# Block 0's rows turned by VectorE, two indirect writes in unit 20, earlier table steps, and the last x's transposes between up products

## The chip, the cores and the metric

The kernel runs on one core of one Trainium2 chip. The metric is the device time of one execution in microseconds (us), from the runs' own clock; a profile of one more execution gives the trace. A core has TensorE (matrix products and transposes, results in PSUM), VectorE and ScalarE (which read and write SBUF and PSUM), GpSimd (SBUF only; it also issues the indirect DMAs) and SyncE, whose queue issues all the direct DMAs. In the rows they are PE, DVE, ACT, POOL and SP.

## What is computed

Two steps follow each other. The first is a linear attention with a decaying state (B=4, H=8, S=768, D=48), computed in the kernel chunk by chunk:

```
for t in range(S):
    cur = einsum('bhd,bhe->bhde', u[None] * kt, vt)
    y[:, :, t] = einsum('bhd,bhde->bhe', rt, state + cur)
    state = wt[:, :, :, None] * state + einsum('bhd,bhe->bhde', kt, vt)
x = y.transpose(0, 2, 1, 3).reshape(3072, 384)
```

The second is a mixture of experts over the 3072 rows of x (8 experts, 384 to 1024 to 384), each row going to one expert:

```
logits = x @ w_gate + modality_bias[modality_id]
e_idx = argmax(logits, axis=1);  gate_w = softmax(logits)[e_idx]
for e in range(E):
    h = maximum(x[mask] @ w1[e], 0.0)
    out[mask] = gate_w[mask, None] * (h @ w2[e])
```

## The kernel before

**Attention.** The 3072 rows are 24 units of 128. A loop `for i in range(-2, NU)` (NU = 24) is a hand-made pipeline: iteration i prepares unit i+2 (decay products B and E, then K and G), makes the scores of unit i+1 (`pS`, masked into `A`) and the result of unit i (`pY`, in the last iteration `pU`). `x_rows(n)` adds `dV` and writes unit n's rows into `xp`; `x_cols(n)` transposes them on TensorE into `pT` or `pK`, from where ScalarE copies them to `xT`; `logits(n)` multiplies by w_gate into the PSUM tile `T["R"]` (`pR_x` in the rows). The program is written out by hand: each engine works through its instructions in the order in which the code issues them, and waits by semaphores.

**Routing.** The rows are routed in two parts, units 0 to 9 (while attention still runs) and 10 to 23. Once the places of the first part are known, `hook_b(0)` puts ten scatters into `pend`, and `drain(1)` issues one indirect write of 128 rows into the DRAM buffer `xs` at the end of each iteration on GpSimd's queue. `table(0)` is a generator whose steps, small operations on VectorE within `pR_x`, find out which expert the blocks 0 and 1 belong to; `hooks` call its steps (`tb`) at the end of the last two iterations.

**Blocks.** The experts' work runs over blocks of 512 rows. `rows_load(q)` loads a block's rows from `xs` into `xl`; for block 0 this is one DMA with 128 rows on the partitions, and its wait is for the last scatter of the first part. In the last iteration `blk_t(0)` turns block 0 by twelve transposes of TensorE into `pX`, `pK` and `pY`, ScalarE casts each third to `xh` and VectorE makes the remainder `xo = x - xh`, since each fp32 product is made of three fp32r products (`xh·wh`, `xo·wh`, `xh·wl`). Blocks from 1 on come by four DMAs of 32 partitions and are turned by VectorE (`rows_turn`, a 32x32 stream transpose) into `xt` in SBUF. The weights of the first expert are split the same way: `w_split_half` casts an eighth's half on ScalarE to `wh` and makes `wl` on GpSimd, sixteen pieces of 128x192 in all. `blk_up(q, f)` is one of eight up products, nine matmuls into a PSUM bank, followed by relu on ScalarE (`h`) and its remainder on VectorE; block 0 uses the two banks `pS0` and `pS1` in turn, later blocks three (`pS0`, `pS1`, `pT`). `blk_down` follows with 72 matmuls. Work of the second routing part stands between the products of block 0, `logits(NU - 1)` after the third (`s == 2`).

Of the kernel before, what the change touches and what calls it, by code (L numbers as in the profile page):

```python
# [18 lines left out]
P = 128  # L19
# [41 lines left out]
def kernel(ctx: ExitStack, tc: tile.TileContext, rkw, vt, wf, cst, mid, wg, bias, w1, w2, out):  # L61
# [223 lines left out]
    SPLITS = {NU - 2: 4, NU - 1: 8}  # L285
    BY_TWO = (1, 2, 7, 8, 9, 10, 11)

    def att_iter(i):
# [21 lines left out]
        if ok(z - 1):  # L310
            x_rows(z - 1, i in BY_TWO)
        last = first(m + 1)
# [78 lines left out]
        if i == NU - 1:  # L391
            x_rows(z)
            blk_t(0)
            x_cols(z, pt(("x", 1), "pT"))
            logits(z - 1)
        if i >= NU - 2:
            hooks.pop(0)()
# [260 lines left out]
    def rows_load(q, at, nj):  # L658
# [4 lines left out]
        if q == 0:  # L663
            nc.sync.dma_start(out=xl.rearrange("p a c -> p (a c)").rearrange("p (j c) -> p j c", j=JT),
                              in_=src[:, 0:DM].rearrange("(j p) c -> p j c", p=P))
        for i in range(4 if q else 0):
            nc.sync.dma_start(out=xl[32 * i:32 * i + 32, 0:4 * nj], in_=src[:, XC * i:XC * i + XC].rearrange("(b t) c -> t b c", t=32))
# [8 lines left out]

    def blk_t(q):
        w = width(q)
        X["x", q] = [bp["m"].tile([P, KC, BT], dt, tag=nm, name=f"{nm}{q}", bufs=1) for nm, dt in (("xh", F32R), ("xo", F32R), ("xt", F32))]
        if q == 0:  # L680
            bp["m"].tile([P, 56], F32, name="pad1")
        xg = X["xg", q]
        xh, xo, xt = ([t[:, m, 0:w] for m in range(KC)] for t in X["x", q])
        if q == 0:
            xl = X["xl", q].rearrange("p a c -> p (a c)").rearrange("p (j k m) -> p j m k", j=JT, m=KC)
            xt = [pt(f"x0_{m}", t) for m, t in enumerate(("pX", "pK", "pY"))]
            for m in range(KC):
                for j in range(JT):
                    nc.tensor.transpose(out=xt[m][:, j * P:(j + 1) * P], in_=xl[:, j, m], identity=ident)

        def rest(m):
            nc.vector.tensor_tensor(out=xo[m], in0=xt[m], in1=xh[m].bitcast(F32), op=ALU.subtract)

        for m in range(KC):
            if q:
                rows_turn(q, m, w // 32, xt[m])
            nc.scalar.copy(out=xh[m], in_=xt[m])
            if m:
                rest(m - 1)
        rest(KC - 1)  # L700
        nc.vector.reciprocal(out=xg[:, :, 0:1], in_=xg[:, :, 0:1])
# [480 lines left out]
```

## Time and profile before

| | |
|---|---|
| timed runs | median 333.74 us, 333.08 to 336.19 (3 runs) |
| the profiled execution | 332.86 us, of which the span (first to last instruction) 331.1 us |
| TensorE busy | 319.8 us, 97% of the span |
| VectorE, ScalarE, GpSimd busy | 222.0, 204.0 and 195.0 us: 67, 62 and 59% |
| granted TensorE clock | 0.999 of full speed |
| DMA | 66.22 MB, mean 200 GB/s |

Attention takes the first 120 us of the span, then come the blocks. Times in the rows are us from the span's start; a matmul row's duration contains the pipeline, so the work of one is read from the distance to the next row's start. Short transfers of 512 B and less make up 27569 of 48321 DMA packets.

### The profile page before, as it was taken

The page shows a single profiled execution, that of the slowest core. Times are in us where ns is not written, and L with a number is a line of the kernel's source. Part 1 is how long each engine was busy: PE and PEld are TensorE (multiplying, and loading weights), DVE is VectorE, ACT ScalarE, POOL GpSimd, SP SyncE. Part 2 cuts the span into 40 slices and gives each one's busy share as a digit, 9 for nine tenths or more (in the row PEclk, how much of TensorE's full clock was granted, in tenths as well). Part 3 has the DMA queues.
Part 4 walks back from the last instruction along what each step waited for, and adds up shares of the span by engine and source line. Part 5 has one row for each costly group of instructions (what it writes and reads, how often), then busy time and mean ns, then how long its engine had stood idle before and what let it go on. Part 6 is the DMA issues. An engine that isn't in the chain of part 4 may idle for free. (4 is left out here: it accounts for less than half of the span.)

```text
span 331.1 us, 9946 instructions
## 1 busy us (share of the span) xinstructions
PE 319.8 (97%) x3831; PEld 279.6 (84%) x3831; DVE 222.0 (67%) x382; ACT 204.0 (62%) x466; POOL 195.0 (59%) x226
## 2 busy tenths in 40 slices
PE   8899999999899999999999999999999999999993
PEld 3688999889799897888888888888888999889993
DVE  6999999899999746777514995874472465353220
ACT  3898799677588875642314748637775786524240
POOL 7998889879999975575435550652056233604041
PEclk9999999999999999999999999999999999999999
DMA  7998889967998532514778128945996594332011
GB/s 267 414 332 263 272 295 258 302 229 246 303 287 277 183 97 89 104 72 173 238 236 213 51 69 201 375 144 131 325 259 262 146 342 157 78 104 78 0 70 56
DMA packets 48321, 66.22 MB, mean 200 GB/s; under 512 B 27569, under 2 KB 34825, under 8 KB 48264
## 3 DMA queue, kind: packets, MB, share of 16 engines
q1 hardware_dynamic: 45160, 56.02, 55.0%
q0 software_dynamic: 3104, 9.47, 7.4%
q8 instruction: 32, 0.52, 0.6%
q14 instruction: 25, 0.20, 0.2%
HBM read 61.65 MB, written 16.46 MB: 236 GB/s over the span
## 5 line engine op out<-in xcount | busy, mean ns | idle before, releaser
L760 POOL DMA_INDIRECT out<-ot,xg x24 | 25.3, 1054 | 72.2 <-ACT ot L772 67.7
L228 ACT CAST wh<-raw 128x768 fp32r<-128x768 f32 x48 | 39.0, 830 | 32.3 <-PE pK_d L730 16.3
L229 POOL TENSOR_TENSOR wl<-raw,wh 128x768 fp32r<-128x768 f32 x20 | 38.8, 1953 | 28.5 <-ACT wh L228 28.4
L717 DVE SCALAR_TENSOR_TENSOR h<-pS_u,h 128x512 fp32r<-128x512 f32 (+1 forms) x34 | 22.9, 674 | 36.1 <-ACT h L716 30.9
L229 DVE TENSOR_TENSOR wl<-raw,wh 128x768 fp32r<-128x768 f32 x28 | 31.0, 1113 | 15.2 <-ACT wh L228 14.5
L711 PE MATMUL pS_u<-xh,wh 128*128 128x512 f32 (+1 forms) x102 | 39.7, 390 | 0.2 <-DVE h L717 0.2
L711 PE MATMUL pS_u<-xo,wh 128*128 128x512 f32 (+1 forms) x102 | 39.2, 384 | 0.0
L711 PE MATMUL pS_u<-xh,wl 128*128 128x512 f32 (+1 forms) x102 | 39.1, 384 | 0.0
L716 ACT ACTIVATE h<-pS_u 128x512 fp32r<-128x512 f32 (+1 forms) x34 | 19.8, 582 | 26.6 <-PE pS_u L711 22.5
L641 POOL DMA_INDIRECT xs<-xp,posT x24 | 24.5, 1022 | 11.2 <-issue 8.2
L246 POOL TENSOR_TENSOR K<-in,B 128x512 f32<-128x512 f32 x24 | 28.4, 1185 | 4.2 <-PE pK L321 2.3
L307 POOL TENSOR_TENSOR G<-in 128x512 f32<-128x512 f32 x24 | 30.6, 1274 | 0.0
L730 PE MATMUL pY_d<-h,wh 128*128 128x512 f32 (+1 forms) x80 | 30.5, 381 | 0.0
L730 PE MATMUL pX_d<-h,wh 128*128 128x512 f32 (+1 forms) x80 | 30.5, 381 | 0.0
L730 PE MATMUL pK_d<-h,wh 128*128 128x512 f32 (+1 forms) x80 | 30.5, 381 | 0.0
L296 DVE TENSOR_TENSOR_SCAN B<-in,pX_d 128x516 f32<-128x516 f32 x24 | 29.3, 1220 | 1.8 <-DMA in<-rkw 1.8
L299 DVE TENSOR_TENSOR_SCAN E<-in,pX_d 128x516 f32<-128x516 f32 x24 | 29.5, 1229 | 0.8
L386 PE MATMUL pY<-v,A 128*64 128x48 f32 x368 | 25.1, 222 | 0.0
L348 DVE TENSOR_TENSOR A<-pS,m 128x768 f32<-128x768 f32 x24 | 22.8, 948 | 2.9 <-PE pS L346 2.7
L252 ACT ACTIVATE pU_st<-pU_st,B 128x48 f32<-128x48 f32 x80 | 22.0, 275 | 3.0 <-PE pU_st L358 0.5
L386 PEld LDWEIGHTS pY<-v,A 128*64 128x64 f32 x368 | 23.7, 138 | 0.0
L346 PEld LDWEIGHTS pS<-R,K 64*64 64x64 f32 x768 | 18.6, 133 | 5.1 <-issue 4.2
(248 smaller groups left out, 829.6 us busy)
## 6 DMA issues: line engine op xcount, KB each, us to landing
raw<-w SPq DMA_DIRECT2D x24, 768.0 KB
in<-rkw SPq DMA_DIRECT2D x23, 512.0 KB
v<-vt SPq DMA_DIRECT2D x24, 288.0 KB
in<-rkw SPq DMA_DIRECT2D x23, 258.5 KB
wg<-wf SPq DMA_DIRECT2D x8, 576.0 KB
xl<-xs SPq DMA_DIRECT2D x20, 192.0 KB
raw<-w SPq DMA_DIRECT2D x16, 192.0 KB
yd<-yt SPq DMA_DIRECT2D x16, 192.0 KB
```

The source lines that it names most:

```text
L228: nc.scalar.copy(out=wh[k][:, sl], in_=raw[k][:, sl])
L229: (eng or (nc.vector, nc.gpsimd)[k]).tensor_tensor(out=wl[k][:, sl], in0=raw[k][:, sl], in1=wh[k][:, sl].bitcast(F32), op=ALU.subtract)
L246: nc.gpsimd.tensor_tensor(out=wt(a, "K", [P, 4, P]), in0=quarters(k), in1=quarters(T["B", a][:, 1:517])[:, :, 1:129], op=ALU.mult)
L296: nc.vector.tensor_tensor_scan(out=Bt[:, 516:0:-1], data0=w[:, 516:0:-1], data1=d1[:, 516:0:-1], initial=0.0, op0=ALU.mult, op1=ALU.max)
L299: nc.vector.tensor_tensor_scan(out=Et, data0=w[:, 0:516], data1=d1[:, 1:2].to_broadcast([P, 516]), initial=1.0, op0=ALU.mult, op1=ALU.max)
L307: nc.gpsimd.tensor_tensor(out=wt(a, "G", [P, 512]), in0=r, in1=k, op=ALU.mult)
L386: nc.tensor.matmul(out=yh[64:P, g, sw, hh], lhsT=A[:, hh, g, 1 + sw], rhs=vs[:, g, hh] if sw else v[:, h * D:(h + 1) * D], start=new and n ...
L641: rows_apart("xs", nc.gpsimd.indirect_dma_start(out=xs[:, :], out_offset=bass.IndirectOffsetOnAxis(ap=posT[:, n:n + 1], axis=0), in_=T["xp ...
L711: nc.tensor.matmul(out=pp, lhsT=wsrc[0][:, f, c * P:(c + 1) * P], rhs=xsrc[:, c], start=(n == 0), stop=(n == 3 * KC - 1))
L717: nc.vector.scalar_tensor_tensor(out=hl, in0=pp, scalar=0.0, in1=hh.bitcast(F32), op0=ALU.max, op1=ALU.subtract)
L730: nc.tensor.matmul(out=X["y", q][c][:, 0:width(q)], lhsT=wsrc[1][:, f, c * P:(c + 1) * P], rhs=hsrc, start=(first and n == 0), stop=(last ...
L760: ins = nc.gpsimd.indirect_dma_start(out=out[:, :], out_offset=bass.IndirectOffsetOnAxis(ap=xg[0:n, j, 1:2].bitcast(I32), axis=0), in_=ot[ ...
```

## The change

Five edits. (1) `rows_load(0)` uses the four DMAs of the other blocks, and block 0 is turned by VectorE in the last iteration, with the casts, three of the weight pieces and the remainders in a new order (`blk_x` takes `blk_t`'s parts apart). (2) Iteration 20 (`NU - 4`) issues two scatters, iteration 21 none. (3) The table's step 1 is called at the end of iteration 21, step 2 in iteration 22 ahead of the mask, the rest at the end of iteration 23. (4) The x columns and logits of unit 23, and the logits of unit 22, stand between the up products of block 0; up products of block 0 use three banks. (5) In the last iteration three weight pieces instead of eight stand ahead of the rest, and the splits for block 1's first weights are made after the up products 2, 3, 5 and 7 instead of 1, 3, 5 and 7.

```diff
-    SPLITS = {NU - 2: 4, NU - 1: 8}
+    SPLITS = {NU - 2: 4}
...
-        if ok(z - 1):
+        if i == NU - 1:
+            b0 = blk_x(0)
+            for c in range(KC):
+                if c == KC - 1:
+                    x_rows(z - 1)
+                rows_turn(0, c, NXB, b0.xt[c])
+                if c == KC - 1:
+                    for _ in range(3):
+                        w_split_half(next(done))
+                b0.cast(c)
+            for c in range(KC):
+                b0.rest(c)
+        elif ok(z - 1):
             x_rows(z - 1, i in BY_TWO)
+            if i == NU - 2:
+                next(tb)
...
             x_cols(z - 1, pt(("x", 0), "pT"))
-        if i == NU - 1:
             x_rows(z)
-            blk_t(0)
-            x_cols(z, pt(("x", 1), "pT"))
-            logits(z - 1)
-        if i >= NU - 2:
+            b0.gate()
             hooks.pop(0)()
...
-        if q == 0:
-            nc.sync.dma_start(out=xl.rearrange("p a c -> p (a c)").rearrange("p (j c) -> p j c", j=JT),
-                              in_=src[:, 0:DM].rearrange("(j p) c -> p j c", p=P))
-        for i in range(4 if q else 0):
+        for i in range(4):
             nc.sync.dma_start(out=xl[32 * i:32 * i + 32, 0:4 * nj], in_=src[:, XC * i:XC * i + XC].rearrange("(b t) c -> t b c", t=32))
...
+    class blk_x:
...
+        def cast(self, m):
+            nc.scalar.copy(out=self.xh[m], in_=self.xt[m])
+        def rest(self, m):
+            nc.vector.tensor_tensor(out=self.xo[m], in0=self.xt[m], in1=self.xh[m].bitcast(F32), op=ALU.subtract)
+        def gate(self):
+            nc.vector.reciprocal(out=self.xg[:, :, 0:1], in_=self.xg[:, :, 0:1])
...
-        pp = pt(f"u{q}_{f}", UPB[(ORDER.index(q) * FC + f) % 3] if isinstance(q, int) and q else f"pS{f % 2}", (P, BT))[:, 0:width(q)]
+        pp = pt(f"u{q}_{f}", UPB[(ORDER.index(q) * FC + f) % 3] if isinstance(q, int) else f"pS{f % 2}", (P, BT))[:, 0:width(q)]
...
-        if i >= NU - 2:
-            hooks.append(lambda n=1 + 2 * (i == NU - 1): [next(tb, None) for _ in range(n)])
+        if i in (NU - 3, NU - 1):
+            hooks.append((lambda: next(tb)) if i < NU - 1 else lambda: list(tb))
...
-        drain(1)
+        drain(2 if i == NU - 4 else 1)
...
-            if s == 2:
-                logits(NU - 1)
+            if s == 0:
+                x_cols(NU - 1, pt(("x", 1), "pT"))
+            if s in (1, 2):
+                logits(NU - 3 + s)
...
-            if q != 1 and f % 2 and nxt < HO:
+            if q > 1 and f % 2 and nxt < HO:
                 w_split(0, f // 2)
+            if q == 0 and f in (2, 3, 5, 7):
+                w_split(0, f // 2 - (f == 2))
```

How the instructions stand now, at three places. VectorE before, from the mask of unit 23 to the first step-2 operation (xp is x_rows, the five operations on pR_x and hd are the table's step 1, xo are the remainders of block 0 read from PSUM):

```order
L348 TENSOR_TENSOR A_2626<-pS_2627,m_111 128x768
L522 TENSOR_SCALAR pR_x<-pR_x 128x8
...
L526 SCALAR_TENSOR_TENSOR pR_x<-one_153,pR_x 128x8
L423 TENSOR_TENSOR xp_1426<-pY_2657,dV_2609 128x384
L423 TENSOR_TENSOR xp_1426<-pU_2718,dV_2699 128x384
L692 TENSOR_TENSOR xo_2753<-pX_x_0_2756,xh_2752 128x512
L692 TENSOR_TENSOR xo_2753<-pK_x_1_2757,xh_2752 128x512
L692 TENSOR_TENSOR xo_2753<-pY_x_2_2758,xh_2752 128x512
L701 RECIPROCAL xg_2597<-xg_2597 128x4
L578 TENSOR_SCALAR fs_2690<-pR_x 128x9
```

VectorE now, from the x rows of unit 21 on (fs to t2 is step 2, xt is block 0 turned in SBUF):

```order
L433 TENSOR_TENSOR xp_1426<-pY_2580,dV_2497 128x384
L588 TENSOR_SCALAR fs_2572<-pR_x 128x9
...
L561 TENSOR_TENSOR t2(0, 1)_2633<-pR_x,t2(0, 1)_2633 128x1
L362 TENSOR_TENSOR A_2650<-pS_2651,m_111 128x768
L679 STREAM_TRANSPOSE xt_2719<-xl_2604 128x512 x2
L433 TENSOR_TENSOR xp_1426<-pY_2681,dV_2620 128x384
L679 STREAM_TRANSPOSE xt_2719<-xl_2604 128x512
L697 TENSOR_TENSOR xo_2718<-xt_2719,xh_2717 128x512 x3
L433 TENSOR_TENSOR xp_1426<-pU_2737,dV_2715 128x384
L700 RECIPROCAL xg_2605<-xg_2605 128x4
L564 SCALAR_TENSOR_TENSOR pR_x<-pR_x,t2(0, 1)_2633 128x1
```

Step 2 moved ahead of the mask A, and the turning ahead of the x rows of units 22 and 23. TensorE before, from the logits of unit 21 to the first up product:

```order
L439 MATMUL pR_x<-cs,xT_2673 64x8 x6
L433 MATMUL pT_('x', 0)_2745<-cs,xp_1426 128x128 x3
L689 MATMUL pX_x_0_2756<-cs,xl_2596 128x128 x4
L689 MATMUL pK_x_1_2757<-cs,xl_2596 128x128 x4
L689 MATMUL pY_x_2_2758<-cs,xl_2596 128x128 x4
L433 MATMUL pT_('x', 1)_2778<-cs,xp_1426 128x128 x3
L439 MATMUL pR_x<-cs,xT_2746 64x8 x6
L711 MATMUL pS_u_0_2872<-xh_2752,wh_74 128x512
L711 MATMUL pS_u_0_2872<-xo_2753,wh_74 128x512
```

TensorE now, the same place up to the third up product:

```order
L449 MATMUL pR_x<-cs,xT_2697 64x8 x6
L443 MATMUL pT_('x', 0)_2764<-cs,xp_1426 128x128 x3
L720 MATMUL pS_u_0_2851<-xh_2717,wh_74 128x512
...
L720 MATMUL pS_u_0_2851<-xh_2717,wl_75 128x512
L443 MATMUL pT_('x', 1)_2864<-cs,xp_1426 128x128 x3
L720 MATMUL pS_u_1_2872<-xh_2717,wh_74 128x512
...
L720 MATMUL pS_u_1_2872<-xh_2717,wl_75 128x512
L449 MATMUL pR_x<-cs,xT_2765 64x8 x6
L720 MATMUL pT_u_2_2891<-xh_2717,wh_74 128x512
```

The twelve transposes are gone, the last x's transposes stand behind the first up product, and the logits of unit 22 behind the second. ScalarE before, from the copy of unit 21's x on (xh are the casts of block 0, wh the weight pieces, h the first relu):

```order
L434 COPY xT_2673<-pK_2672 128x384
L234 CAST wh_74<-raw_72 128x192 x8
L434 COPY xT_2746<-pT_('x', 0)_2745 128x384
L697 CAST xh_2752<-pX_x_0_2756 128x512
L697 CAST xh_2752<-pK_x_1_2757 128x512
L697 CAST xh_2752<-pY_x_2_2758 128x512
L434 COPY xT_2779<-pT_('x', 1)_2778 128x384
L234 CAST wh_74<-raw_72 128x192 x4
```

ScalarE now:

```order
L444 COPY xT_2697<-pK_2696 128x384
L694 CAST xh_2717<-xt_2719 128x512 x2
L234 CAST wh_74<-raw_72 128x192 x3
L694 CAST xh_2717<-xt_2719 128x512
L444 COPY xT_2765<-pT_('x', 0)_2764 128x384
L234 CAST wh_74<-raw_72 128x192 x9
```

Three weight casts stand between the second and the third cast of block 0, nine behind, and the first relu follows those nine.

## Rows read from the trace of the kernel before

**Rows 1.** Windows, one stretch: its length, then busy us of each engine

```profile
131.00:326.00 195.00, 195.00 (x951) 169.68 (x949) 105.95 (x200) 102.66 (x165) 80.63 (x79) 1.00 0.55 167
```

**Rows 2.** Timeline of TensorE, 116 to 131: start, us, engine, line, operation, idle before

```profile
116.79 0.50 PE L439 MATMUL pR_x<-cs,xT 128*64 128x8 f32 x12
...
119.16 0.25 PE L383 MATMUL pU<-vz,A 128*64 128x96 f32 x1
...
120.68 0.55 PE L433 MATMUL pT_('x', 0)_2745<-cs,xp 128*128 128x128 f32 x3
121.06 0.62 PE L689 MATMUL pX_x<-cs,xl 128*128 128x128 f32 x4
...
122.43 0.49 PE L433 MATMUL pT_('x', 1)_2778<-cs,xp 128*128 128x128 f32 x3
...
123.30 0.50 PE L711 MATMUL pS_u<-xh,wh 128*128 128x512 f32 x1
123.64 0.40 PE L711 MATMUL pS_u<-xo,wh 128*128 128x512 f32 x1
...
127.93 0.50 PE L711 MATMUL pS_u<-xh,wh 128*128 128x512 f32 x1 [0.21 <-DVE h L717]
...
129.87 0.39 PE L711 MATMUL pS_u<-xh,wl 128*128 128x512 f32 x1
...
130.64 0.50 PE L711 MATMUL pS_u<-xh,wh 128*128 128x512 f32 x1
```

**Rows 3.** Timeline of VectorE, 113 to 127

```profile
113.94 0.56 DVE L423 TENSOR_TENSOR xp<-pY,dV 128x384 f32<-128x384 f32 x1 [1.13 <-PE pY L386]
115.22 0.96 DVE L348 TENSOR_TENSOR A<-pS,m 128x768 f32<-128x768 f32 x1 [0.72 <-PE pS L346]
...
124.22 0.14 DVE L578 TENSOR_SCALAR fs<-pR_x 128x9 f32<-128x9 f32 x1
...
126.45 0.16 DVE L551 TENSOR_TENSOR t2(0, 1)_2792<-pR_x,t2(0, 1)_2792 128x1 f32<-128x1 f32 x1
```

**Rows 4.** Timeline of GpSimd, 107 to 114: two indirect writes into xs

```profile
107.83 1.01 POOL L641 DMA_INDIRECT xs<-xp,posT  x1 [0.16 <-DVE A L348]
...
112.23 1.01 POOL L641 DMA_INDIRECT xs<-xp,posT  x1 [0.17 <-issue]
```

**Rows 5.** Timeline of SyncE's queue: the loads of block 0 and of block 1

```profile
115.41 0.39 SPq L664 DMA_DIRECT2D xl<-xs  x1
...
134.22 1.97 SPq L667 DMA_DIRECT2D xl<-xs  x4
```

**Rows 6.** DMA queues (packets, MB, share): q0 in 112:113, q1 in 138:139

```profile
q0 software_dynamic: 9, 0.02, 5.9%
...
q1 hardware_dynamic: 852, 0.16, 112.6%
```

**Rows 7.** Timeline of VectorE, 144 to 146: turning block 1

```profile
144.14 1.63 DVE L672 STREAM_TRANSPOSE xt<-xl 128x512 f32<-128x512 f32 x2
145.69 0.69 DVE L692 TENSOR_TENSOR xo<-xt,xh 128x512 fp32r<-128x512 f32 x1
```

**Rows 8.** Timeline of GpSimd and of VectorE, 187 to 190, weight remainders on both

```profile
187.47 2.56 POOL L229 TENSOR_TENSOR wl<-raw,wh 128x768 fp32r<-128x768 f32 x1
...
188.25 2.59 DVE L229 TENSOR_TENSOR wl<-raw,wh 128x768 fp32r<-128x768 f32 x1
...
189.99 2.56 POOL L229 TENSOR_TENSOR wl<-raw,wh 128x768 fp32r<-128x768 f32 x1
```

**Rows 9.** Timeline of GpSimd, 118 to 129: weight pieces, then one alone

```profile
118.73 4.47 POOL L235 TENSOR_TENSOR wl<-raw,wh 128x192 fp32r<-128x192 f32 x8 [1.30 <-ACT wh L234]
...
127.15 1.84 POOL L229 TENSOR_TENSOR wl<-raw,wh 128x768 fp32r<-128x768 f32 x1 [0.89 <-ACT wh L228]
```

**Rows 10.** Timeline of ScalarE, 118 to 127: weight casts and the first relu

```profile
118.31 2.12 ACT L234 CAST wh<-raw 128x192 fp32r<-128x192 f32 x8
...
125.75 0.60 ACT L716 ACTIVATE h<-pS_u 128x512 fp32r<-128x512 f32 x1 [1.09 <-POOL wl L235]
```

More of the change, by code (lines that the diff above doesn't have):

```diff
@@ L675, in blk_load, with __init__ @@
         rows_load(q, q if at is None else at, JT)
-    def blk_t(q):
[L678 to L692, printed above, removed]
+    class blk_x:
+        def __init__(self, q):
+            w = width(q)
+            X["x", q] = [bp["m"].tile([P, KC, BT], dt, tag=nm, name=f"{nm}{q}", bufs=1) for nm, dt in (("xh", F32R), ("xo", F32R), ("xt", F32))]
+            if q == 0:
+                bp["m"].tile([P, 56], F32, name="pad1")
+            self.xg = X["xg", q]
+            self.xh, self.xo, self.xt = ([t[:, m, 0:w] for m in range(KC)] for t in X["x", q])
+        def cast(self, m):
[4 more added lines that the diff above has]
+            nc.vector.reciprocal(out=self.xg[:, :, 0:1], in_=self.xg[:, :, 0:1])
+    def blk_t(q):
+        b = blk_x(q)
         for m in range(KC):
-            if q:
-                rows_turn(q, m, w // 32, xt[m])
-            nc.scalar.copy(out=xh[m], in_=xt[m])
+            rows_turn(q, m, width(q) // 32, b.xt[m])
+            b.cast(m)
             if m:
-                rest(m - 1)
-        rest(KC - 1)
-        nc.vector.reciprocal(out=xg[:, :, 0:1], in_=xg[:, :, 0:1])
+                b.rest(m - 1)
+        b.rest(KC - 1)
+        b.gate()
     UPB = ("pS0", "pS1", "pT")
```

## The prediction

> **What bounds the kernel now.** I read the page's engine totals first. TensorE is busy 97% of the span, the other three between 59 and 67%, as the table above has it. Averages can hide a stage, so the second view is a single long stretch: from 131 to 326 us TensorE is busy 195.00 of 195.00 us [rows 1]. Everything behind the change, from the fourth up product of block 0 to the last product, is one gapless chain on TensorE. Whatever moves the start of that fourth product (130.64 us before) moves the end by as much, as long as the other engines keep up. So the question is at what time it starts now.
>
> The third view is TensorE's timeline around the hand-over from attention to block 0 [rows 2]. The reader should see hardly an idle time there: after the last attention unit come the transposes of x of unit 22 (120.68), the twelve transposes that turn block 0 (three groups of four, the first at 121.06), the transposes of x of unit 23 (122.43), twelve small logits products, and the first up product at 123.30. One wait stands in the rows, 0.21 us before the third up product, for VectorE to free a PSUM bank. TensorE is bound by its own work here. The change can win only what it takes off TensorE, and loses where it makes TensorE wait.
>
> **The change, part by part, on TensorE.** All times are on the trace's clock.
>
> (a) The twelve turning transposes go: 121.06 to 122.43, 1.37 us off.
>
> (b) With three banks in turn, the third up product no longer waits for the first bank. That is 0.21 us, and 0.1 us of restart: the step from the first to the second matmul of a product that follows something else is 0.34 us (123.30 to 123.64), within a product it is (129.87 - 127.93)/8 = 0.24. Together 0.3 off.
>
> (c) The last x's transposes and the logits of unit 22 stood before the up products and took 0.87 us (122.43 to 123.30). Now they stand between products. The trace has one such insertion, the logits of unit 23: the last matmul of a product begins at 129.87, the next product at 130.64, 0.77 us where 0.24 would do. With the restart an insertion costs 0.63. The transposes take 0.38 (120.68 to 121.06) where the logits take the other 0.49 of the 0.87, so theirs costs 0.52. Sum 1.15 against 0.87: 0.3 added.
>
> (d) Step 2 of the table moves ahead of the mask of unit 23 (A<-pS) on VectorE. The first of its twelve small operations began at 124.22 and the last ended at 126.45 + 0.16: 2.39 us [rows 3]. It now follows the x rows of unit 21, which end at 113.94 + 0.56 = 114.50, so it ends at 116.89, and the mask at 117.85 instead of 116.18. The product that reads the mask begins at 119.16 [rows 2]: 1.3 us of cover, no cost. But the logits of unit 20, due at 116.79, write the PSUM tile that the table works in, and in the new order they wait for step 2: 0.1 us and the hand-over, between 0.1 and 0.3. I take 0.2, and all of TensorE's work behind it shifts. Step 1 (five such operations, about 1.0 us) now stands ahead of the x rows of unit 21, where VectorE idled 1.13 us [rows 3]: no cost; if it overran by 0.1, only those rows would be later by it.
>
> (e) The second indirect write in unit 20 puts 1.01 us [rows 4] on GpSimd ahead of dV, K and G of the next unit. The write at 112.23 is gone in turn, so GpSimd is level again at 113.2, and G, which ended at 112.06 before that write, now ends at 113.1. K is out a G's length earlier, and the products that read it end only when the mask starts, 115.22 [rows 3]; G is read behind them. No cost. Without the cover of the missing write it would be 1.0 us.
>
> So (a) to (d) make -1.37 - 0.3 + 0.3 + 0.2 = -1.17 us. The first up product would start at 120.68 + 0.2 + 0.4 = 121.3, its second matmul at 121.6, its fifth at 122.35, its eighth at 123.05. These three read the remainders xo of the three thirds of x.
>
> **Is block 0 turned in time?** This is VectorE's work now, and it begins with the load. Before, the last write left GpSimd at 112.23 + 1.01 and the load was issued at 115.41 [rows 4, 5], 2.17 us later. The new last write leaves GpSimd near 109.9, but then the weight loads still hold the DMA engines: the write issued at 107.83 was still moving packets after 112 [rows 6], 3.5 us later. The new one queues behind it, with 0.2 MB more, so it lands near 113.1 and the load is issued near 113.5. Bounds: 112.1 (the unloaded 2.17 us) and 115.41 (as before). The load now has the form of block 1's: issued at 134.22, moving until somewhat before 139 [rows 5, 6], 4.5 us. So it lands near 118.05 (116.6 to 119.9), and the first turn starts at 118.15, hardly later than the mask allows.
>
> From block 1's rows two turns take 1.63 us, so one each 0.78, and a subtraction 0.69 [rows 7]. With the x rows of unit 22 (0.56) between, the third turn ends at 121.0, and the first subtraction could start at 120.94.
>
> Here stands what I hold for the decisive row. These subtractions now read both operands from SBUF; before, one came from PSUM. At the same time GpSimd makes the weight remainders, also from two SBUF operands. Where both engines did this side by side, near 188 us, they took turns: one on GpSimd stretched to 2.56 us and one on VectorE to 2.59, begun 2.52 us after the one before [rows 8], while GpSimd alone takes 1.84 [rows 9]. So 0.68 us of a 768 wide one on VectorE is added to GpSimd's time; for 512 wide that is 0.45. GpSimd's pieces here are 128x192, 4.47/8 = 0.56 each [rows 9], so a pair takes 1.02 instead of VectorE's own 0.60. The second third is turned at 119.75; its cast, about 0.6 like the relu, and the first of the weight casts (2.12/8 = 0.27 each) [rows 10] let GpSimd begin at 120.75, 0.2 before the first subtraction. Then the subtractions end at 121.9, 122.9 and 123.9 and the eighth matmul waits till 124.0 instead of 123.05: 1.0 us lost. If VectorE comes first, 0.6. If the two don't meet, 0.1. I take 0.8.
>
> The Trainium skill, page SBUF — State Buffer, section Who interferes with whom, states that a VectorE instruction with two SBUF inputs and a GpSimd one that reads SBUF exclude each other for the whole instruction. By that a pair would take 0.56 + 0.69 = 1.25 us, the last subtraction would end about 0.5 later, and the sum below would be +0.13 instead of -0.37. The trace's row agrees on the turns, but its pair is 2.52 and not 1.84 + 0.96; I go by the row.
>
> What comes behind holds: the x rows of unit 23 end at 124.4, TensorE wants them at 124.55. On ScalarE nine weight casts now stand ahead of the first relu, and the copy of the last x behind both: from 122.3 they take 9 x 0.27 + 0.60 + about 0.5, so the copy ends near 125.8. The third up product needs its bank at 127.7. That is 2 us of cover; with it gone, each us would count.
>
> **Sum.** -1.17 + 0.8 = -0.37 us on 332.86, the profiled execution's own time (span 331.1 and 1.8 around it): 332.5. The median of the timed runs is 0.9 above that execution and the lowest 0.2; from the median it would be 333.4. I give 332.9.
>
> **Rivals.**
> *The turn is in time and undisturbed (0.25).* For it: the meeting hangs on 0.2 us of ScalarE's order, and the load may land at 116.6. Then the loss is 0.1 and the sum -1.07: 331.8 from its own time, 332.2 on the middle base.
> *The load lands late, slower than before (0.2).* Each us past the 118.15 taken delays turns, casts, subtractions and TensorE by one us. From 118.5 on the kernel is slower. At the bound (issued at 115.41 as before) the first turn is at 120.0: -0.37 + 1.85 = +1.5, 334.4. For it speaks the queueing of the write at 107.83; against it, that the write of before, with the engines free, needed 2.17 us and the new one has 5.5 until that bound.
> *Whole instructions exclude each other (0.1).* A pair then takes 0.56 + 0.69 = 1.25, the last subtraction ends 0.5 later than in the forecast and the sum is +0.13: 333.0 from its own time. Against it stands the pair of 2.52 where 1.84 and VectorE's own time would make more.
> *The change doesn't do what it says (0.05):* the work taken off TensorE before 131 us is won only if the engines behind keep up with an earlier chain, and nothing in one execution shows their slack to a us; the sum then ends at 332.9 from its own time.
>
> The forecast itself has 0.4, between -0.6 and -0.1 us. All cases lie inside 1% (3.3 us), which is about what a measurement can tell from no change here: removing everything in (a) to (b) is 1.7 us, and the late load is capped at +1.5. I leave 0.04 for faster and 0.07 for slower by more than that, for what I haven't seen. The range reaches from the undisturbed case with half a us of scatter, 331.2, to the late load on the upper base, 335.0.
>
> **What would show it.** In the profile after: no turning transposes on TensorE, the first up product near 121.3 and the fourth near 130.3. Logits of unit 20 with a short wait for VectorE. The new load issued near 113.5: at 112 the queueing was wrong, at 115 the late load is right. The subtractions of block 0 near 1.0 us apart and longer than 0.69: the engines take turns; 0.6 apart: they don't. Waits of TensorE for VectorE inside the first up product of about 0.8 us. The forecast is wrong if TensorE waits somewhere after 131 us, or if the third up product waits for the copy of the last x.

## The result and the profile after

The changed kernel takes 335.31 us (median of 22 runs, 333.83 to 339.36), the kernel before, timed beside it, 333.39 (22 runs, 332.41 to 336.35). The ratio is 1.0055, 95% interval [1.0037, 1.0073]: slower by 1.9 us. The forecast was 0.4 us faster, with 332.9 and a range up to 335.0; both the sign and the range missed.

The first lines of the page of the kernel after say how little the averages tell. TensorE is as busy as before (319.9 us, 319.8 before) in a span that is 2.7 us longer. TensorE's last product ends 2.12 us later (328.20, before 326.08), the other 0.6 us lies behind it:

```profile
span 333.8 us, 9932 instructions
...
PE 319.9 (96%) x3818; PEld 278.5 (83%) x3819; DVE 226.1 (68%) x385; ACT 204.0 (61%) x466; POOL 196.2 (59%) x226
```

From the fourth up product of block 0 on nothing has changed. A window of 195 us (columns: length, busy us of each engine, granted clock, DMA share, GB/s) is as gapless as in [rows 1], only 2 us later:

```profile
133.00:328.00 195.00, 195.00 (x951) 169.75 (x950) 107.61 (x201) 103.52 (x167) 80.75 (x80) 1.00 0.55 167
```

So the loss lies ahead of it, as the prediction had placed it. Timeline of TensorE around the hand-over, kernel after (start, duration, engine, line, operation, idle time before and who ended it):

```profile
114.79 0.55 PE L443 MATMUL pT<-cs,xp 128*128 128x128 f32 x3
...
117.90 0.52 PE L449 MATMUL pR_x<-cs,xT 128*64 128x8 f32 x12 [0.46 <-DVE t2(0, 1)_2633 L561]
...
122.81 0.55 PE L443 MATMUL pT_('x', 0)_2764<-cs,xp 128*128 128x128 f32 x3 [0.93 <-DVE xp L433]
...
124.49 0.50 PE L720 MATMUL pS_u<-xo,wh 128*128 128x512 f32 x1 [0.90 <-DVE xo L697]
...
130.05 0.50 PE L720 MATMUL pT_u<-xh,wh 128*128 128x512 f32 x1
...
132.76 0.50 PE L720 MATMUL pS_u<-xh,wh 128*128 128x512 f32 x1
```

The reader should see two new waits for VectorE: 0.93 us for the x rows of unit 22 and 0.90 us for the first remainder xo. Neither is in [rows 2]. The fourth up product starts at 132.76 where it was at 130.64. That is 2.12 us, as much as TensorE's last product moved. One measure of the hand-over is the distance from the first row to the fourth up product. That row is the transposes of x of unit 20, issued in iteration 22 (the expectations below call it the first transposes of unit 23); where it starts is taken as the end of the units. Before, it is this one:

```profile
113.77 0.55 PE L433 MATMUL pT<-cs,xp 128*128 128x128 f32 x3
```

The distance is 132.76 - 114.79 = 17.97 us after and 130.64 - 113.77 = 16.87 before, 1.10 us more; the units ended 1.02 us later in this one execution. But that lateness is no second loss. VectorE waits for the load below, and the load waits for the indirect writes, not for the units' end: it is issued at 114.28 here and at 114.22 in e2, whose units end 1.01 us sooner. Where the load is late, units that end sooner only wait longer, so there the start of the fourth up product itself is the measure, and the loss is the whole 2.12 us.

VectorE, the same stretch, shows who is late:

```profile
117.77 0.95 DVE L362 TENSOR_TENSOR A<-pS,m 128x768 f32<-128x768 f32 x1
120.67 1.65 DVE L679 STREAM_TRANSPOSE xt<-xl 128x512 f32<-128x512 f32 x2 [1.96 <-DMA xl<-xs]
122.24 0.52 DVE L433 TENSOR_TENSOR xp<-pY,dV 128x384 f32<-128x384 f32 x1
122.67 0.88 DVE L679 STREAM_TRANSPOSE xt<-xl 128x512 f32<-128x512 f32 x1
123.48 2.96 DVE L697 TENSOR_TENSOR xo<-xt,xh 128x512 fp32r<-128x512 f32 x3
```

VectorE stood still for 1.96 us until block 0's load had landed. Behind the first two turns stand the x rows of unit 22, for which TensorE waits, and the three remainders, which take 2.96 us together where three undisturbed ones take 1.84 (e2). The load itself, in SyncE's queue, and the two writes on GpSimd that it waits for, with the three of GpSimd's weight pieces that run beside the remainders:

```profile
114.28 2.76 SPq L674 DMA_DIRECT2D xl<-xs  x4
```

```profile
107.75 1.01 POOL L651 DMA_INDIRECT xs<-xp,posT  x1
109.06 0.97 POOL L651 DMA_INDIRECT xs<-xp,posT  x1 [0.30 <-issue]
...
123.30 2.59 POOL L235 TENSOR_TENSOR wl<-raw,wh 128x192 fp32r<-128x192 f32 x3 [5.40 <-ACT wh L234]
```

From issue (114.28) to the first turn (120.67) it is 6.39 us. The windows of 1 us show that most bytes had moved by 119 (the last two columns are the DMA share and GB/s):

```profile
118.00:119.00 1.00, 1.00 (x20) 0.81 (x21) 0.71 (x1) 0.06 (x1) 0.00 (x0) 1.00 1.19 252
119.00:120.00 1.00, 1.00 (x32) 1.00 (x32) 0.00 (x0) 0.41 (x1) 0.00 (x0) 1.00 0.39 35
```

The trace's single packets say it more exactly. The load is 2048 packets of 384 B, and the last of them ended at 119.74, 5.46 us behind the issue and 0.93 us ahead of the turn.

### The profile page after: what moved, and what is told of

Its sections match the earlier page's. It is cut to its first block, busy times and chain, and to the rows that moved or that the text cites. A ratio compares the mean times of both kernels' runs of the same rounds, so it can differ in the third digit from the quotient of the medians.

```text
span 333.8 us, 9932 instructions
## 1 busy us (share of the span) xinstructions
PE 319.9 (96%) x3818; PEld 278.5 (83%) x3819; DVE 226.1 (68%) x385; ACT 204.0 (61%) x466; POOL 196.2 (59%) x226
## 5 line engine op out<-in xcount | busy, mean ns | idle before, releaser
L726 DVE SCALAR_TENSOR_TENSOR h<-pS_u,h 128x512 fp32r<-128x512 f32 (+1 forms) x32 | 21.5, 672 | 34.8 <-ACT h L725 34.7
L229 DVE TENSOR_TENSOR wl<-raw,wh 128x768 fp32r<-128x768 f32 x28 | 32.0, 1149 | 15.3 <-ACT wh L228 14.7
L720 PE MATMUL pS_u<-xo,wh 128*128 128x512 f32 (+1 forms) x96 | 37.1, 387 | 1.0 <-DVE xo L697 0.9
L720 PE MATMUL pS_u<-xh,wh 128*128 128x512 f32 (+1 forms) x96 | 37.4, 389 | 0.0
L720 PE MATMUL pS_u<-xh,wl 128*128 128x512 f32 (+1 forms) x96 | 36.8, 384 | 0.0
L725 ACT ACTIVATE h<-pS_u 128x512 fp32r<-128x512 f32 (+1 forms) x32 | 18.6, 581 | 23.4 <-PE pS_u L720 21.5
L694 ACT CAST xh<-xt 128x512 fp32r<-128x512 f32 (+1 forms) x18 | 10.9, 607 | 18.6 <-DVE xt L679 17.9
```

The costliest lines, as they stand in the source:

```text
L229: (eng or (nc.vector, nc.gpsimd)[k]).tensor_tensor(out=wl[k][:, sl], in0=raw[k][:, sl], in1=wh[k][:, sl].bitcast(F32), op=ALU.subtract)
L720: nc.tensor.matmul(out=pp, lhsT=wsrc[0][:, f, c * P:(c + 1) * P], rhs=xsrc[:, c], start=(n == 0), stop=(n == 3 * KC - 1))
```

## The experiments

Theory L: all of the loss comes from the first block's load being late, which holds VectorE at the first turn. Its rivals: GpSimd's pieces and VectorE's remainders taking turns (already in the forecast at 0.8 us), step 2 of the table ahead of the mask, the second write in unit 20, and the work put between the up products. The table collects all runs; "hand-over" is the distance defined above and "fourth" the start of the fourth up product. These come from one profiled execution each, which in e9 and e11 was the slowest of twelve, with late units, and in e4 the fastest of six. The ratio is to the kernel before, timed beside it.

| kernel | unit 20's transposes at | fourth at | hand-over, us | median, us | ratio |
|---|---|---|---|---|---|
| before | 113.77 | 130.64 | 16.87 | 333.39 | 1 |
| after | 114.79 | 132.76 | 17.97 | 335.31 | 1.0055 [1.0037, 1.0073] |
| e1 rows from the input | 113.70 | 130.26 | 16.56 | 333.67 | 1.0005 [0.9976, 1.0033] |
| e2 pieces early | 113.78 | 131.29 | 17.51 | 334.98 | 1.0047 [1.0016, 1.0079] |
| e3 step 2 late | 113.07 | 132.75 | 19.68 | 335.69 | 1.0072 [1.0043, 1.0100] |
| e4 one write each | 113.06 | 133.41 | 20.35 | 338.09 | 1.0143 [1.0107, 1.0178] |
| e5 before, two writes | 113.15 | 130.03 | 16.88 | 333.02 | 0.9991 [0.9970, 1.0013] |
| e6 before, work between | 113.52 | 130.47 | 16.95 | 334.10 | 1.0018 [0.9993, 1.0043] |
| e7 input, seven pieces early | 113.05 | 129.24 | 16.19 | 332.70 | 0.9978 [0.9952, 1.0004] |
| e8 writes early | 113.50 | 130.79 | 17.29 | 333.55 | 1.0005 [0.9981, 1.0028] |
| e9 writes and pieces early | 116.87 | 133.36 | 16.49 | 333.43 | 1.0004 [0.9977, 1.0030] |
| e10 writes earlier, four pieces | 114.87 | 130.23 | 15.36 | 333.97 | 1.0016 [0.9991, 1.0040] |
| e11 input, four pieces | 117.35 | 132.72 | 15.37 | 332.48 | 0.9965 [0.9943, 0.9986] |
| e12 writes early, four pieces | 115.10 | 130.26 | 15.16 | 333.51 | 0.9995 [0.9972, 1.0018] |

### e1: the load has nothing to wait for

```diff
-  in_=src[:, XC * i:XC * i + XC].rearrange(...)
+  in_=(vt[0:nj * P] if q == 0 else src)[:, XC * i:XC * i + XC].rearrange(...)
```

> The changed kernel, but block 0's rows are read from the kernel's input v instead of from xs, at the same place in the queue; so the load waits for no indirect write (block 0 then computes on other rows). Theory L (the load lands too late: first turn at 120.67 after 1.96 us of idle VectorE): the first turn follows the mask at 118.7, the x rows of unit 22 no longer hold TensorE (0.93 us), the first remainder no longer (0.90): 1.8 to 2.1 us less than the changed kernel, level with the kernel before (ratio 0.999 to 1.001). Rival T (the engines' taking turns at the remainders is the loss): that stays, so at most 0.9 less, ratio about 1.003. Rival W (two writes in one unit slow the units): no change, 1.0055.

Measured: 333.67 us, 1.0005, 1.6 us less than the change. SyncE's queue, then VectorE, then TensorE of this kernel:

```profile
110.30 2.93 SPq L674 DMA_DIRECT2D xl<-vt  x4
```

```profile
118.10 1.72 DVE L679 STREAM_TRANSPOSE xt<-xl 128x512 f32<-128x512 f32 x2 [0.49 <-DMA xl<-vt]
...
120.97 2.98 DVE L697 TENSOR_TENSOR xo<-xt,xh 128x512 fp32r<-128x512 f32 x3
```

```profile
113.70 0.55 PE L443 MATMUL pT<-cs,xp 128*128 128x128 f32 x3
...
120.71 0.55 PE L443 MATMUL pT_('x', 0)_2764<-cs,xp 128*128 128x128 f32 x3
...
122.00 0.50 PE L720 MATMUL pS_u<-xo,wh 128*128 128x512 f32 x1 [0.51 <-DVE xo L697]
...
130.26 0.50 PE L720 MATMUL pS_u<-xh,wh 128*128 128x512 f32 x1
```

The load was issued 4 us sooner, the first turn began at 118.10 (the forecast had 118.15), though VectorE still waited 0.49 us for the load, and TensorE no longer waits for the x rows. The fourth up product starts at 130.26; the forecast had 130.64 - 0.37 = 130.27. The hand-over took 16.56 us, 0.31 less than before. With the first turn at the time that the prediction gave it, what the prediction says of the way behind the turn holds. The late load is the loss: 132.76 - 130.26 = 2.50 us at the fourth up product, 1.41 by the hand-over, and 1.6 timed.

### e2: no weight pieces beside the remainders

```diff
-    SPLITS = {NU - 2: 4}
+    SPLITS = {NU - 2: 4, NU - 1: 7}
...
-                    for _ in range(3):
-                        w_split_half(next(done))
```

> The changed kernel, but seven weight pieces stand at the head of the last iteration, where GpSimd idled 5.4 us, and none between the casts. Theory L with T as its second part: the turn stays at 120.7, the remainders of block 0 step by 0.6 instead of 1.0, so the eighth matmul of the first up product comes at 125.4 instead of 126.5: 0.9 to 1.1 less than the changed kernel, ratio to before about 1.0025. If L alone counted: no change, 1.0055. If T alone counted: 1.8 less, 1.000.

Measured: 334.98 us, 1.0047. VectorE, then TensorE:

```profile
120.14 1.65 DVE L676 STREAM_TRANSPOSE xt<-xl 128x512 f32<-128x512 f32 x2 [2.44 <-DMA xl<-xs]
```

```profile
131.29 0.50 PE L717 MATMUL pS_u<-xh,wh 128*128 128x512 f32 x1
```

The remainders now run 0.6 us apart (1.84 us for three, 2.96 in the change), and from the first turn to the fourth up product it takes 11.15 us where the change takes 12.09 (120.67 to 132.76): 0.94 us less in the traces. The load is as late as in the change: TensorE waited 1.42 us for the x rows of unit 22. Timed, only 0.3 us were gained; the intervals hold no gain as well as one of 0.9.

### e3: step 2 of the table behind the mask

```diff
-            if i == NU - 2:
-                next(tb)
```

> The changed kernel, but step 2 of the table is not called ahead of the mask; it runs with the other steps at the end of the last iteration. The wait of the logits of unit 20 for step 2 (0.46 us in the trace) goes. Rival S (that wait is part of the loss): 0.5 less than the changed kernel, ratio 1.004. Theory L: TensorE gets earlier to the x rows of unit 22 and waits there for the same late turn, so no change (0.0 to 0.1 less), ratio 1.0055.

Measured: 335.69 us, 1.0072. No gain: TensorE reaches the x rows of unit 22 sooner and waits there longer, 1.96 us. The wait of 0.46 us for step 2 in the change was covered by the late load. In this execution the units ended 1.72 us sooner than in the change's and the load was issued 0.95 sooner, so that TensorE came to the first remainder 1.24 us sooner. Yet the fourth up product starts at the same time (132.76 in the change):

```profile
123.25 0.50 PE L718 MATMUL pS_u<-xo,wh 128*128 128x512 f32 x1 [0.90 <-DVE xo L695]
...
132.75 0.50 PE L718 MATMUL pS_u<-xh,wh 128*128 128x512 f32 x1
```

That stretch takes 9.50 us where the change takes 8.27 and e1 8.26, and the windows of TensorE say why (length, busy, granted clock, DMA):

```profile
122.00:124.00 2.00, 1.10 (x6) 1.00 0.00 0
124.00:126.00 2.00, 1.96 (x6) 0.63 0.00 0
126.00:128.00 2.00, 2.00 (x8) 0.52 0.00 0
128.00:130.00 2.00, 2.00 (x20) 1.00 0.00 0
```

After its waits TensorE was granted about half its full clock, the 1.2 GHz level, for some 3 us. There matmuls of an up product start 0.43 us apart, at the full clock 0.23. That cost 1.23 us.

### e4: one write per unit again, as before

```diff
-        drain(2 if i == NU - 4 else 1)
+        drain(1)
```

> The changed kernel with one indirect write per unit as before, so the last one comes a unit later. Theory L: the load is issued about 1.1 to 2 us later than at 114.28 and the first turn with it, so 1 to 2 us more than the changed kernel, ratio 1.009 to 1.011. Rival W: the units before run as in the kernel before, 0.5 to 1.0 less than the changed kernel, ratio about 1.003.

Measured: 338.09 us, 1.0143, 2.8 us more than the change, more than expected. In the profiled execution the load was issued at 114.80, only 0.5 us later than in the change, and the first turn came at 120.72, as there. The units were 1.7 us ahead, so VectorE waited 3.75 us for the load and TensorE 2.68:

```profile
122.82 0.55 PE L443 MATMUL pT_('x', 0)_2764<-cs,xp 128*128 128x128 f32 x3 [2.68 <-DVE xp L433]
...
124.50 0.80 PE L720 MATMUL pS_u<-xo,wh 128*128 128x512 f32 x1 [0.90 <-DVE xo L697]
...
133.41 0.50 PE L720 MATMUL pS_u<-xh,wh 128*128 128x512 f32 x1
```

```profile
124.00:126.00 2.00, 1.50 (x4) 0.50 0.00 0
126.00:128.00 2.00, 2.00 (x10) 0.67 0.00 0
```

Theory L holds in direction: a later load, a longer time, so the second write in unit 20 did help the change. From the first remainder on (124.50, in the change 124.49) this execution lost 0.65 us, with 0.50 and 0.67 of the clock granted right after the wait: there a late load was paid for twice, once by the wait and once by the clock behind it. The profiled execution is the fastest of the six, 2.1 us under their median; what the others lost no profile shows.

### e5 and e6: two parts of the change alone, on the kernel before

```diff
-        drain(1)
+        drain(2 if i == NU - 4 else 1)
```

> The kernel before with one edit: two indirect writes in unit 20 and none in unit 21. Block 0 is still loaded at the same place and turned by TensorE. Theory L (all of the loss comes from block 0's rows landing late): nothing changes at the end of the units, ratio 1.000, between 0.998 and 1.002; TensorE's first transposes of unit 23 start where they did, within 0.3 us, since GpSimd does the same work by the end of unit 21. Rival W (the second write itself costs): GpSimd's rows in the units stand back to back (4.42 us of work in a unit of 4.42 us), so 1.2 us more of it in unit 20 delay the products of v, K and G of unit 21, and the units end 0.6 to 1.2 us later: ratio 1.002 to 1.004.

Measured: 333.02 us, 0.9991; the hand-over is 16.88, unit 20's transposes start at 113.15. GpSimd's rows do stand back to back, and the second write pushes dV as far as feared:

```profile
107.42 1.01 POOL L641 DMA_INDIRECT xs<-xp,posT  x1 [0.17 <-issue]
108.73 0.98 POOL L641 DMA_INDIRECT xs<-xp,posT  x1 [0.30 <-issue]
109.71 0.86 POOL L303 TENSOR_TENSOR dV<-v,dT 128x384 f32<-128x384 f32 x1
```

But the units end on time, and the timed interval leaves 0.4 us at most. Rival W falls for one extra write.

The second kernel puts the last x's transposes and logits between the up products and gives block 0 three banks:

```diff
-            x_cols(z, pt(("x", 1), "pT"))
-            logits(z - 1)
...
-  ... if isinstance(q, int) and q else f"pS{f % 2}", ...
+  ... if isinstance(q, int) else f"pS{f % 2}", ...
...
-            if s == 2:
-                logits(NU - 1)
+            if s == 0:
+                x_cols(NU - 1, pt(("x", 1), "pT"))
+            if s in (1, 2):
+                logits(NU - 3 + s)
```

> The kernel before with two parts of the change alone: the last x's transposes and the logits of units 22 and 23 go between the up products of block 0, and block 0's up products take three banks in turn. Block 0's rows are still turned by TensorE and nothing else moves. The prediction's terms (b) -0.3 us for the third bank and (c) +0.3 us for the insertions cancel: ratio 1.000, between 0.998 and 1.002; the wait of 0.21 us before the third up product is gone. Rival: the insertions cost more than a bank gives, and part of the change's loss comes from here: ratio 1.002 to 1.004, with waits of TensorE at the inserted places.

Measured: 334.10 us, 1.0018 with an interval that holds 1; the hand-over is 16.95 instead of 16.87 and the wait before the third up product is gone. In its place TensorE waits 0.23 us for the first remainder, which the earlier first up product now reaches too soon. Terms (b) and (c) cancel to within 0.1 us in the trace, that wait included. The timed interval can't exclude a cost of up to 1.4 us.

### e7 and e11: what taking turns costs by itself

Both load block 0 from the input, as e1, and differ from it in GpSimd's pieces: seven at the head of the last iteration (e7), or four (e11), and the others behind block 0's casts.

```diff
-    SPLITS = {NU - 2: 4}
+    SPLITS = {NU - 2: 4, NU - 1: 7}        # e11: 4
...
-                    for _ in range(3):
-                        w_split_half(next(done))
```

> The change with block 0's rows loaded from the input v, not from the sorted rows that the writes fill (so the rows turned are others, and the load does not wait for the writes), and with seven of GpSimd's pieces at the head of the last iteration, none between the turns. The load is in time, as in the run that only loads from the input (333.67 us, ratio 1.0005), and no GpSimd row runs beside block 0's differences. If the two engines' taking turns is a price of its own, as the prediction has it (0.8 us), the differences start 0.6 us apart where they were 1.0, and the time is 0.8 us below that run: ratio 0.998 to the kernel before, and from TensorE's first transposes of unit 23 to the fourth up product 15.8 us where that run had 16.56. Rival: the differences were no longer what the up products wait for, and the time stays at 1.0005.

> The change with block 0's rows loaded from the input v (so the rows turned are others, and nothing waits for the writes) and four of GpSimd's pieces at the head of the last iteration, eight after block 0's casts. It differs from the run that only loads from the input in GpSimd's pieces alone. If taking turns at the differences has the price that the prediction gives it (0.8 us), the differences start 0.6 us apart (1.0 there), unit 23's first transposes to the fourth up product take 15.8 us (16.56 there), and the ratio is 0.997 to 0.998 (1.0005 there). If not, 16.5 us and 1.000.

Measured: e7 332.70 us, 0.9978; e11 332.48, 0.9965 [0.9943, 0.9986], 1.2 us below the kernel before. In e7 the remainders begin as early as in e1 and GpSimd still works through its pieces beside them (2.77 us for three), so its gain is partial. In e11 GpSimd is through with four pieces while the second remainder runs. VectorE, then TensorE of e11:

```profile
124.06 2.26 DVE L694 TENSOR_TENSOR xo<-xt,xh 128x512 fp32r<-128x512 f32 x3
```

```profile
117.35 0.55 PE L440 MATMUL pT<-cs,xp 128*128 128x128 f32 x3
...
132.72 0.50 PE L717 MATMUL pS_u<-xh,wh 128*128 128x512 f32 x1
```

The hand-over is 15.37 us where e1 has 16.56, 1.19 less, and timed 1.3 less (0.0040 of 333.5, with intervals that overlap). Not all of it need be the pieces: in e1 VectorE waited 0.49 us for the load, and its first turn comes 4.40 us behind the transposes of unit 20, in e11 3.84 without a wait. So the pieces beside the remainders cost between 0.6 and 1.2 us here, 0.94 by e2 against the change; the forecast had 0.8. Without them the sum comes to 15.37 - 16.87 = -1.50 in the trace, -1.2 timed; the forecast's (a) to (d) were -1.17.

### e8, e9, e10, e12: the same with the real rows

Here the load is made timely by earlier writes. Two writes each go out in units 18 and 19 (e8, e9), in 15 to 17 (e10) or in 17 and 18 (e12), and the load stays at its place. e9 has seven pieces at the head, e10 and e12 four.

```diff
-        drain(2 if i == NU - 4 else 1)
+        drain(2 if i in (NU - 6, NU - 5) else 1)   # e10: NU - 9, NU - 8, NU - 7; e12: NU - 7, NU - 6
```

> The change with its second write moved: two writes each in units 18 and 19, so that the tenth is out in unit 19 and the first block's load (at its place behind the weight loads of SP's queue) has nothing to wait for. Theory L: the load is issued at about 110 us, the first turn starts when VectorE is free, at about 118, TensorE does not wait for the last x rows, and the time is that of the run that loaded from the input: ratio 1.000 (0.998 to 1.003), some 1.5 us below the change. Rival W: GpSimd is 2.5 us behind after unit 19 and catches up only by unit 21; if that slows the units, the first transposes of unit 23 start up to 1.2 us later and the gain is eaten: ratio 1.004.

> The change with both repairs: two writes each in units 18 and 19 (none in 20 and 21), and seven of GpSimd's pieces at the head of the last iteration, none between block 0's turns. Theory L with taking turns as a price of its own: the sum of the prediction without its two losses, -1.17 us or a little less, 332.5 us, ratio 0.997, below the kernel before and the change. If only the late load mattered: 1.000. If the early writes slow the units (rival W): 1.003.

> The change with both repairs carried further: two writes each in units 15, 16 and 17 (the tenth is out in unit 18), so the first block's load has nothing to wait for behind the weight loads, and only four of GpSimd's pieces at the head of the last iteration, the other eight after block 0's casts, so that GpSimd is idle or done while VectorE takes block 0's differences. Theory: load issued at about 110 us, first turn at about 118 with no late wait, the three differences 0.6 us apart, TensorE from unit 23's first transposes to the fourth up product in 15.8 us (17.97 in the change, 16.87 before): ratio 0.997, about 1 us below the kernel before. Rival (the late load only, taking turns no price): 16.5 us and ratio 1.000.

> The change with two writes each in units 17 and 18 (the tenth is out in unit 19), and four of GpSimd's pieces at the head of the last iteration, eight after block 0's casts. It differs from the run with writes in units 15 to 17 in how far GpSimd falls behind: two extra writes (2.5 us), not three (3.7 us), by the time the units catch up. In the run with three, the hand-over took 15.36 us (16.87 before) but the units ended 1.1 us later and the time was 1.0016 of the kernel before; in the run with two extra writes (units 18 and 19) the units ended on time. Theory: the units end on time (first transposes of unit 23 at 113.1 to 113.8), the load is issued at about 111, the first turn starts at about 117.5, and the hand-over takes 15.4 to 15.8 us: ratio 0.996 to 0.997, 332.3 us. Rival: GpSimd's lag costs the units already with two extra writes, or the load is still late: ratio 1.000 or above.

Measured: 333.55, 333.43, 333.97 and 333.51 us, all within 0.2% of the kernel before; the 0.996 to 0.997 expected of e9, e10 and e12 did not come. In e8 the second write of unit 19 ended at 106.80 and the load was issued at 112.22, not at 110: under the weight loads that write needed 5.4 us. The first turn came at 118.64, TensorE waited 0.27 us for the x rows and 0.90 us for the first remainder, and the hand-over is 17.29, between the change and e1. All four lie below the change. e8 differs from it in the writes alone, 1.0005 [0.9981, 1.0028] against 1.0055 [1.0037, 1.0073], so the late load is confirmed with the real rows too.

e12 shows the hand-over as it was hoped for. SyncE, VectorE, TensorE:

```profile
109.86 1.95 SPq L671 DMA_DIRECT2D xl<-xs  x4
```

```profile
118.93 1.70 DVE L676 STREAM_TRANSPOSE xt<-xl 128x512 f32<-128x512 f32 x2
...
121.82 1.86 DVE L694 TENSOR_TENSOR xo<-xt,xh 128x512 fp32r<-128x512 f32 x3
```

```profile
115.10 0.55 PE L440 MATMUL pT<-cs,xp 128*128 128x128 f32 x3
...
130.26 0.50 PE L717 MATMUL pS_u<-xh,wh 128*128 128x512 f32 x1
```

No wait of VectorE for the load, three remainders in 1.86 us (here a GpSimd piece that began 0.02 us behind the first of them took 2.30 us and let all three pass; in e11 such a piece took 1.08 us and the second remainder as long), and 15.16 us from the first row to the last, 1.71 less than before. Yet the fourth up product starts at 130.26, only 0.38 sooner than before, and the time is that of before. In the profiled executions of e10 and e12 the units ended 1.1 and 1.3 us later than before. For e10 one row of the waits names GpSimd, in 85 to 115 us (columns: who, for whom, us in total, times, longest):

```profile
PE pR_x L446 <- issue: 0.9, 1, 0.9
PE pK L332 <- POOL K L246: 0.5, 1, 0.5
```

Three extra writes (0.97 us each with 0.30 ahead) put GpSimd some 3.8 us behind, and TensorE waited 0.5 us for K. The larger waits there, and those of e12, are "issue": TensorE waited for nothing that the profile shows. Such waits are in the units of every execution here, in other places and sizes (2.3 us at once in e9, 1.0 before), so one profile can't tell what of them comes from the early writes; e11, without early writes, ended its units later still. Against e11 (0.9965), e12 is 0.0030 slower, with intervals that overlap. That the units give back what the hand-over gains fits these numbers, but it isn't shown. No version with the real rows was faster than the kernel before by a measurable amount.

## Why the prediction was wrong

**What bounds the kernel: right.** The stretch behind the fourth up product is as gapless as before, and TensorE's last product moved by as much as that product's start. TensorE did not wait after 131 us, nor the third up product for the copy of the last x, the two signs of a wrong forecast that the prediction named.

**(a) to (c): right, with (c) a little dear.** The twelve transposes are gone, and e6 has the third bank and the insertions at +0.08 us together where the forecast had 0.0. In the change the second up product starts 0.50 us behind the last matmul of the first (126.83 to 127.33), so the transposes between them cost 0.26 us; the forecast had 0.52. That and a smaller (d) account for the step from -1.17 to e11's -1.50.

**(d) step 2 ahead of the mask: right.** In e8 the distance from the transposes of unit 20 to those of unit 21 (pK, 117.06 - 113.50) is 3.56, before 3.45 (117.22 - 113.77): 0.1 us, the lower of its two bounds. In the change the distance is the same, with a wait of 0.46 for step 2 in the place of one for ScalarE; without either it is 3.00 in e3, but under the late load that brings nothing.

**(e) the second write: right.** e5 has it at 0.9991, and e4 shows that the load would be later without it.

**The turn, its start: here it failed.** The first turn was forecast at 118.15 and came at 120.67, 2.52 us later. Two terms made that time. The issue of the load was forecast at 113.5, between 112.1 and 115.41, and came at 114.28: 0.78 late, inside its bounds. The second write left GpSimd at 110.03 (forecast 109.9), and its last packet ended at 113.80 where the forecast had 113.1.

The landing was forecast 4.5 us behind the issue, read from block 1's load as "moving until somewhat before 139" [rows 5, 6]. It was 6.39 us in the change, 5.92 to 6.14 in e2 to e4; this term, 1.7 of the 2.52 us, is the one that was mis-sized. It was too small in two ways. A window in which packets move does not show the last one: block 1's load, with the same 2048 packets, ended at 139.16, 4.94 us behind its issue, and the change's 5.46 us behind. And the end of the packets is not the time at which a reader may start: the turn began 0.93 us behind the last one in the change, and 0.67 to 0.88 us behind in e1 to e4, e7 and e8, in all of which VectorE waits for the load. The Trainium skill, page DMA: Bandwidth & Descriptors, section Anatomy of one DMA, states for transfers from GpSimd that of some 2 us of fixed cost most lies behind the last byte, since the signal waits until that byte is confirmed. The 0.93 us here, for a transfer from SyncE's queue, agree in kind. The kernel before held the number, in two rows that the prediction didn't use, SyncE's and VectorE's of a later block:

```profile
174.34 2.07 SPq L667 DMA_DIRECT2D xl<-xs  x4
```

```profile
180.34 1.63 DVE L672 STREAM_TRANSPOSE xt<-xl 128x512 f32<-128x512 f32 x2 [2.36 <-DMA xl<-xs]
```

There VectorE waits for the load, and from issue to the first turn it is 6.00 us. Block 1's turn, which the prediction read, had waited for nothing, so it could not tell when its load was ready.

**The late-load rival: its rule right, its cap wrong.** By its rule each us past 118.15 costs one, which gives -0.37 + 2.52 = +2.15 us; the fourth up product moved by +2.12. From the first turn to that product the forecast has 12.12 us and the change 12.09. But the rival, with a chance of 0.2, saw lateness in the write's queueing alone. It took over the 4.5 us, and so put the first turn at 120.0 and the loss at +1.5 at most. Both were exceeded, and with them the upper end of the range.

**Taking turns: right.** The remainders run up to 1.00 us apart in the change where the forecast had 1.02 for a pair, and 0.6 apart in e2 and e12. GpSimd's piece came 0.18 us ahead of the first remainder (forecast 0.2), the case that the forecast priced at 1.0; the traces have 0.94 (e2 against the change), and the mean of its cases, 0.8, was near enough. The "undisturbed" rival fell.

**What is left.** The fourth up product moved by 2.12 us, and the timed loss is 1.9 us, between 1.2 and 2.4, so the late load is enough for it. The profiled execution of the change kept a granted clock of 1.00 through the hand-over. The mean granted clock over the whole of a timed execution has a median of 0.993 in the change, 0.997 in the kernel before, between 0.992 and 0.993 in e3 and 0.989 in e4. That fits with the change paying for the clock too in part of its executions, but no profile of it shows this; it is argued, not shown.

## What to carry to other kernels

To tell when a load is ready, look in the trace for a row in which the reader really waits for that kind of load, and take issue to first use. A window in which packets still move doesn't show the last of them, and the last of them is 0.7 to 0.9 us too early here. Before moving work from the engine that bounds the kernel to one that is nearly free, write down the latest time at which that engine may get its data, and compare it with the latest bound of the load, not with the likely one: here 0.35 us of slack stood against 1.85 us of uncertainty. A difference between two marks in a trace is a measure only if nothing from outside sets the later mark: here the late load did, and the distance from the units' end hid half of the loss. A wait on TensorE can cost more than its length, since the clock can fall behind it (1.23 us in e3, 0.65 in e4).

## What the runs showed that was not expected

After waits of 1.96 us in e3 and 2.68 in e4 in the hand-over, each followed by 0.90 for the first remainder, TensorE's granted clock was at 0.50, the 1.2 GHz level, for some 3 us, with up-product matmuls 0.43 instead of 0.23 us apart. After 0.93 and 0.90 us in the change's profile, and 1.42 and 0.58 in e2's, it stayed at 1.00. In e9 it fell to 0.50 too, from 116 to 119 us, behind a wait of 2.33 us in the units.

A short VectorE instruction can wait for a whole GpSimd one. In e6 the last small operation of the table reads two SBUF operands of 128x8, and meets a weight remainder on GpSimd; VectorE's row, then GpSimd's:

```profile
126.87 1.82 DVE L579 TENSOR_TENSOR fA<-fA,hd 128x8 f32<-128x8 f32 x1
```

```profile
126.83 1.83 POOL L229 TENSOR_TENSOR wl<-raw,wh 128x768 fp32r<-128x768 f32 x1 [1.19 <-ACT wh L228]
```

The operation takes 0.16 us in the kernel after and 1.82 us here, to the end of GpSimd's instruction. This agrees with the Trainium skill, page SBUF — State Buffer, section Who interferes with whom, on the whole-instruction exclusion that the prediction had set aside for its pair of 2.52 us; the pairs are shorter than the two durations added (remainders 0.9 to 1.0 us apart, not 1.25), so the rule holds and adding the durations overstates it.
